# Window attention on two head pairs at once: scores of four heads in quarters of TensorE's array

## The chip, the cores and the metric

The kernel runs on one core of a Trainium2 chip. The metric is the device time of one execution in microseconds. The kernel before takes 718.71 us (median of three runs, 718.19 to 719.21). PE is the matmul engine (TensorE), DVE the vector engine, ACT the scalar engine, POOL the general engine (GpSimd); SP issues most of the DMAs.

## The reference

Three layers in a row: causal attention with a window of 64 positions (4 sequences of 576 positions, 8 heads of 64), a feed-forward layer of 512 to 2048 to 512 for all 2304 tokens, and a second one of 512 to 1024 to 512 with a softmax-weighted activation and a layer norm. All in float32.

```python
scores = q @ k^T / 8                               # per sequence and head, 576 x 576
scores = where(0 <= row - col < 64, scores, -1e9)  # a query sees itself and 63 keys before it
attn = softmax(scores)
x = attn @ v                                       # heads side by side: 2304 x 512
h = x @ w_in                                       # 2304 x 2048
g = where(h >= 1, h, where(h <= -1, 0, (h + 1)**2 / 4))
x = g @ w_out                                      # 2304 x 512
h = x @ w_in2; s = h * softmax(h)
out = layer_norm(s) * g_ln @ w_out2
```

## The kernel before, in words

The attention is worked off in *groups*. A group is a tile of 192 positions (12 tiles, `TT`) and a pair of heads (4 pairs, `NP`), so there are 48 groups, counted by `g`; a group's queries stand in three blocks of 64, and each block sees 128 keys (its own 64 and the 64 before). The first block of a sequence sees 64 keys only (`first`). The stages of a group:

- `st_qkt` brings queries and keys into transposed form, head dimension on the partitions, two heads on 128 partitions. The first three tiles do it with TensorE (L324) and copies out of PSUM (L327 to L329), the others with DVE's transposes from a special DMA layout (L314, L316). The queries are written into `q_diag`, a block-diagonal tile that is zeroed once: 64 columns of the first head filled on the upper 64 partitions, 64 columns of the second on the lower.
- `st_s` multiplies (L342): one product of 128 rows contracted, 128 stationary columns (2 heads x 64 queries) and 128 moving columns (keys) per block. The zeros of `q_diag` keep the heads apart. DVE adds the mask and takes the row's extreme (L350), ACT takes the exponential and its sum (L356).
- `st_norm` divides by the sum (L366 to L375), `st_t` transposes the weights with TensorE (L388, L390) and copies them (L393, L395), `st_v` multiplies with the values (L409): two products of 64 stationary columns per block, one per head, which write the upper and the lower 64 partitions of the output. ACT and DVE split the result into two parts `xh` and `xl` (L416, L417).

A product of float32 operands stands in the trace as two weight loads and two matmuls, here called passes: 144 score products give 288 rows of L342.

The MoE layer goes over blocks of 384 tokens (`j`, 6 blocks) and chunks of 128 hidden units (`f`, 16 chunks): 12 matmuls for a chunk (L429, three products of split operands for four parts of the contraction), the activation (ACT L438, L439, DVE L444, ACT L445, DVE L449), and 12 matmuls for the output two chunks later (L460). The first chunks are done in two halves of 192 tokens so that they can start before the second tile's attention is ready. In the first block the weights are also converted: ACT L130, DVE L134 and L135, ACT L143, POOL L144.

The order of the work: a prologue runs the first groups (`G0` = 6) stage by stage; from then on a generator, `slots`, gives out the attention in quarter steps, two of them per MoE chunk (`slot`). A scheduler then orders each engine's instructions, so that the order on an engine is near to, but not the same as, the order in the code. PSUM has eight banks: four hold the MoE output, and from the second block on the other four are a ring (`at_bank`, `h_bank`) that scores, values, transposes and MoE chunks take in turn.

Of the kernel before, what the change touches and what calls it, by code (L numbers as in the profile page):

```python
# [20 lines left out]
def kernel(  # L21
# [12 lines left out]
    nc = tc.nc  # L34
# [17 lines left out]
    G0, F0, NC, NQ, NV = 6, 2, 4, 6, 7  # L52
# [198 lines left out]
    qn, kn, qk, vw, qT, kT, xh, xl = {}, {}, {}, {}, {}, {}, {}, {}  # L251
    sc, pr, sums, pT = {}, {}, {}, {}

    def load_qk(g):
# [3 lines left out]
        if g < NPE:  # L261
# [10 lines left out]
            for h0, h1 in ((0, 2), (2, H)) if t == 0 else ((0, H),):  # L272
# [8 lines left out]
        for src, r0, m0 in ((q, tl * TT, 0), (k, tl * TT - back, 6)):  # L281
# [19 lines left out]

    q_diag = [at_p.tile([128, QB, 2, 64], F32, bufs=1, name=f"q_diag{z}") for z in range(2)]
    for z in q_diag:
        nc.vector.memset(z, 0.0)

    def st_qkt(g):
        t, hp = divmod(g, NP)
        qt = qT[g] = q_diag[g % 2]
        kt = kT[g] = at_p.tile([128, TT + 64], F32, tag="kT", name="kT")
        if g >= NPE:  # L310
            a = qk.pop(g)
            for x in range(2):
                s_ = slice(64 * x, 64 * x + 64)
                nc.vector.transpose(qt[s_, :, x, :], a[s_, 0:6, :].rearrange("p m c -> p (m c)"))  # L314
            c0 = 0 if t % TPB else 64
            nc.vector.transpose(kt[:, c0:], a[:, 6:14 - c0 // 32, :].rearrange("p m c -> p (m c)"))  # L316
            return
        ps = at_bank("ps_t")
        c = 0
        for src in (qn, kn):  # L320
# [5 lines left out]
        psq = ps[:, 0:TT].rearrange("c (i q) -> c i q", i=QB)  # L326
# [7 lines left out]
    def st_s(g):  # L334
        t, hp = divmod(g, NP)
        ps = at_bank("ps_s")
        tmp = p = at_p.tile([128, QB, 128], F32, tag="p", bufs=3, name="p")
        mx = at_p.tile([128, QB], F32, tag="mx", name="mx")
        sm = at_p.tile([128, QB], F32, tag="sm", name="sm")
# [8 lines left out]
        for i in range(QB):  # L348
            c0 = 64 if first(t, i) else 0
            nc.vector.tensor_tensor_reduce(  # L350
                out=tmp[:, i, c0:], in0=ps[:, i * 128 + c0:i * 128 + 128], in1=mask[:, c0:],
                scale=-0.125, scalar=3.0e38, op0=ALU.add, op1=ALU.min, accum_out=mx[:, i:i + 1],
            )
        for i in range(QB):
            c0 = 64 if first(t, i) else 0
            nc.scalar.activation(  # L356
                p[:, i, c0:], tmp[:, i, c0:], ACTF.Exp, bias=mx[:, i:i + 1], scale=-1.0,
                accum_out=sm[:, i:i + 1],
            )
        pr[g], sums[g] = p, sm  # L360

    def st_norm(g):
        t, hp = divmod(g, NP)
        p, sm = pr[g], sums.pop(g)
# [3 lines left out]
        eng = nc.gpsimd if g < NPE else nc.vector  # L368
# [12 lines left out]
    def st_t(g):  # L381
        t, hp = divmod(g, NP)
        p = pr.pop(g)
# [12 lines left out]
        pT[g] = o  # L396

    def st_v(g):
# [506 lines left out]
```

## Time and profile before

| | |
|---|---|
| time, median of 3 runs | 718.71 us |
| profiled execution, first to last instruction | 717.6 us |
| PE busy | 697.3 us (97%), 4259 matmuls |
| DVE busy | 455.7 us (64%) |
| ACT busy | 417.2 us (58%) |
| POOL busy | 194.3 us (27%) |

The profiled execution's own time is its span of 717.6 us; the median of the runs is 1.1 us longer. A PE that is busy 97% of the time is not at its peak, since a matmul's record runs from its start to the end of its last column while the next one has already begun; the distance between starts is what a matmul costs in a row of its like. The busy shares are means over stages with different limits, so the stages are read apart below.

### The profile page before, as it was taken

The numbers are of one execution on the slowest core, as the hardware profiler recorded it, in microseconds if no ns is written. First come the engines' busy times: TensorE is split into PE (matmuls) and PEld (weight loads), VectorE is DVE, ScalarE is ACT, GpSimd is POOL, SyncE is SP. The second block draws the span as 40 slices with busy tenths as digits, with TensorE's granted clock in tenths as the row PEclk, the third lists the DMA queues.
The fourth block names the chain that finished last, engine by engine and source line by source line (L and its number), as shares of the span: only waits on it lengthen the run. The fifth ranks groups of instructions, "written<-read, shape, count | busy, mean of one in ns | idle before, by whom it ended". The sixth has DMA issues, their size and how long they took to land.

```text
span 717.6 us, 12382 instructions
## 1 busy us (share of the span) xinstructions
PE 697.3 (97%) x4259; PEld 640.5 (89%) x4259; DVE 455.7 (64%) x1222; ACT 417.2 (58%) x1021; POOL 194.3 (27%) x217
## 2 busy tenths in 40 slices
PE   7899889999999999999999999999999999999998
PEld 5689878999999999999999999989998888888887
DVE  4549998564556556655566543463368889988850
ACT  5778877555556555666665655454454645545541
POOL 2458877200002000012002101662274132310000
PEclk9989999999999999999999999999999999999999
DMA  9985897624234252336342200644005445553421
GB/s 197 212 241 174 221 244 178 123 63 106 70 78 138 51 127 56 84 96 152 62 117 92 71 30 31 228 140 147 0 19 186 163 162 176 180 171 109 143 74 44
DMA packets 155542, 88.91 MB, mean 124 GB/s; under 512 B 118616, under 2 KB 141400, under 8 KB 155480
## 3 DMA queue, kind: packets, MB, share of 16 engines
q1 hardware_dynamic: 144040, 64.00, 35.3%
q0 software_dynamic: 8704, 19.41, 8.2%
q10 hardware_dynamic: 2736, 4.72, 1.8%
q8 instruction: 33, 0.54, 0.3%
q14 instruction: 29, 0.24, 0.1%
HBM read 63.97 MB, written 24.12 MB: 123 GB/s over the span
## 4 chain that ended last, share of the span: by engine, by line
PE 80%; issue 7%; DVE 6%; POOL 3%; ACT 2%; DMA 1%; SPq 0%; DVEq 0%; POOLq 0%; ACTq 0%
PE ps_h L429 22%; PE acc L460 22%; PE ps_o L746 14%; PE P L631 10%; PE ps_s L342 5%; PE ps_x L409 4%; PE ps_p L390 2%; POOL wil L247 2%; DVE wst L135 1%; DVE wst L134 1%; DVE gl L449 1%; ACT p L356 1%; PE ps_t L324 1%; DMA qk<-in_q_dram 1%; DVE u L444 0%
## 5 line engine op out<-in xcount | busy, mean ns | idle before, releaser
L429 PE MATMUL ps_h<-xh,wih 128*128 128x384 f32 (+1 forms) x392 | 133.3, 340 | 4.0 <-DVE u L444 4.0
L429 PE MATMUL ps_h<-xl,wih 128*128 128x384 f32 (+1 forms) x392 | 132.1, 337 | 1.4 <-DVE xl L417 1.4
L460 PE MATMUL acc<-gl,woh 128*128 128x384 f32 (+1 forms) x392 | 131.2, 336 | 2.0 <-DVE gl L449 1.6
L429 PE MATMUL ps_h<-xh,wil 128*128 128x384 f32 (+1 forms) x392 | 131.7, 336 | 0.0
L460 PE MATMUL acc<-gh,wol 128*128 128x384 f32 (+1 forms) x392 | 129.8, 333 | 0.0
L444 DVE SCALAR_TENSOR_TENSOR u<-u,ps_h 128x384 f32<-128x384 f32 (+1 forms) x98 | 53.3, 544 | 117.1 <-ACT u L439 116.9
L460 PE MATMUL acc<-gh,woh 128*128 128x384 f32 (+1 forms) x392 | 126.7, 342 | 0.0
L438 ACT ACTIVATE u<-ps_h,half 128x384 f32<-128x384 f32 (+1 forms) x98 | 56.1, 574 | 90.7 <-PE ps_h L429 86.9
L429 PEld LDWEIGHTS ps_h<-xh,wih 128*128 128x128 f32 x392 | 75.1, 192 | 5.6 <-DVE u L444 5.0
L445 ACT CAST gh<-u 128x384 fp32r<-128x384 f32 (+1 forms) x98 | 49.7, 507 | 49.3 <-DVE u L444 40.9
L429 PEld LDWEIGHTS ps_h<-xl,wih 128*128 128x128 f32 x392 | 75.2, 192 | 2.2 <-DVE xl L417 2.0
L460 PEld LDWEIGHTS acc<-gl,woh 128*128 128x128 f32 x392 | 73.8, 188 | 3.7 <-DVE gl L449 2.2
L449 DVE TENSOR_TENSOR gl<-u,gh 128x384 fp32r<-128x384 f32 x80 | 54.4, 680 | 35.1 <-ACT gh L445 34.6
L429 PEld LDWEIGHTS ps_h<-xh,wil 128*128 128x128 f32 x392 | 75.1, 191 | 0.0
L460 PEld LDWEIGHTS acc<-gh,wol 128*128 128x128 f32 x392 | 73.7, 188 | 0.1
L460 PEld LDWEIGHTS acc<-gh,woh 128*128 128x128 f32 x392 | 72.4, 188 | 0.5
L631 PE MATMUL P<-wih,x2p 128*128 128x512 f32 x216 | 70.5, 390 | 0.5 <-DVE xo L472 0.5
L356 ACT ACTIVATE p<-p,mx 128x128 f32<-128x128 f32 (+1 forms) x144 | 55.7, 389 | 17.4 <-DVE mx L350 17.4
L746 PE MATMUL ps_o<-woh,wol 128*128 128x512 f32 (+1 forms) x152 | 57.8, 380 | 0.0
L746 PE MATMUL ps_o<-woh,woh 128*128 128x512 f32 (+1 forms) x152 | 57.7, 379 | 0.0
L746 PE MATMUL ps_o<-wol,woh 128*128 128x512 f32 (+1 forms) x152 | 57.5, 378 | 0.0
L439 ACT ACTIVATE u<-u 128x384 f32<-128x384 f32 (+1 forms) x98 | 51.0, 520 | 2.3
(114 smaller groups left out, 1291.2 us busy)
## 6 DMA issues: line engine op xcount, KB each, us to landing
vw<-in_v_dram SPq DMA_DIRECT2D x32, 256.0 KB, 5.0
wst<-in_moe_w_in_dram SPq DMA_DIRECT2D x16, 512.0 KB, 5.0
wst<-in_moe_w_out_dram SPq DMA_DIRECT2D x16, 512.0 KB, 5.0
lnd<-e SPq DMA_DIRECT2D x16, 512.0 KB, 2.7
lT<-lnd SPq DMA_DIRECT2D x64, 128.0 KB, 2.9
x2d<-xo POOLq DMA_DIRECT2D x24, 192.0 KB, 2.3
out_dram<-o ACTq DMA_DIRECT2D x17, 256.0 KB, 2.8
wst<-in_moe_w_in_dram POOLq DMA_DIRECT2D x8, 512.0 KB, 5.5
```

Of the source, the lines that this page charges most:

```text
L342: nc.tensor.matmul(ps[:, i * 128 + c0:i * 128 + 128], qT[g][:, i, :, :].rearrange("p x q -> p (x q)"), kT[g][:, i * 64 + c0:i * 64 + 128], ...
L356: nc.scalar.activation(p[:, i, c0:], tmp[:, i, c0:], ACTF.Exp, bias=mx[:, i:i + 1], scale=-1.0, accum_out=sm[:, i:i + 1],)
L409: nc.tensor.matmul(ps[64 * x:64 * x + 64, i * 64:i * 64 + 64], vw[t, i][0:n, 2 * hp + x, :], o[0:n, i, 64 * x:64 * x + 64], start=True, st ...
L429: nc.tensor.matmul(ps, a, bb[:, kc, c], start=(n == 0), stop=(n == 3 * KC - 1))
L438: nc.scalar.activation(u, ps, ACTF.Relu, bias=half, scale=0.5)
L439: nc.scalar.activation(u, u, ACTF.Square)
L444: g = nc.vector.scalar_tensor_tensor(u, u, 1.0, ps, op0=ALU.min, op1=ALU.max)
L445: return nc.scalar.copy(hi, u).ins, g.ins
L449: eng.tensor_tensor(lo, u, as_f32(hi), op=ALU.subtract)
L460: nc.tensor.matmul(acc[j, e][:, c], a, bb, start=(f == 0 and n == 0 and c.start == 0), stop=(f == NF - 1 and n == 2),)
L631: nc.tensor.matmul(ps, l, r, start=(n == 0), stop=(n == 5))
L746: nc.tensor.matmul(ps, a[kk // 4][:, kk % 4, :], b[kk][:, c:c + w], start=(n == 0), stop=(n == 3 * NK2 - 1),)
```

## The change

The attention goes over *pairs* of groups: `P` counts 24 of them, each a tile of 192 positions and four heads (two head pairs `c`, two heads `x` in each). `q_diag` is gone. Keys and queries of a group now stand in one tile `kqT` (256 and 192 columns, two heads on 128 partitions), so that DVE transposes them in one instruction. For each block of 64 queries `st_s` issues four products that contract over 64 rows: head `x` has its rows on partitions 64x to 64x + 63, head pair `c` writes PSUM partitions 64c to 64c + 63, and the two `x` write two different PSUM banks. The weights `p` are then kept per `x`, with the two head pairs on the upper and the lower partitions. The values' products of two groups write one bank, and `xh` and `xl` are made for both in one instruction each.

```diff
-    G0, F0, NC, NQ, NV = 6, 2, 4, 6, 7
+    PR0, F0 = 3, 2
...
-            for h0, h1 in ((0, 2), (2, H)) if t == 0 else ((0, H),):
+            for h0, h1 in ((0, 4), (4, H)) if t == 0 else ((0, H),):
...
     def st_qkt(g):
         t, hp = divmod(g, NP)
-        qt = qT[g] = q_diag[g % 2]
-        kt = kT[g] = at_p.tile([128, TT + 64], F32, tag="kT", name="kT")
+        z = kqT[g] = at_p.tile([128, KQ + TT], F32, tag="kqT", name="kqT")
+        c0 = 0 if t % TPB else 64
         if g >= NPE:
             a = qk.pop(g)
-            for x in range(2):
-                s_ = slice(64 * x, 64 * x + 64)
-                nc.vector.transpose(qt[s_, :, x, :], a[s_, 0:6, :].rearrange("p m c -> p (m c)"))
-            c0 = 0 if t % TPB else 64
-            nc.vector.transpose(kt[:, c0:], a[:, 6:14 - c0 // 32, :].rearrange("p m c -> p (m c)"))
+            nc.vector.transpose(z[:, c0:], a[:, c0 // 32:, :].rearrange("p m c -> p (m c)"))
             return
...
-        nc.vector.tensor_copy(qt[0:64, :, 0, :], psq[0:64])
-        nc.scalar.copy(qt[64:128, :, 1, :], psq[64:128])
-        nc.scalar.copy(kt[:, TT + 64 - (c - TT):], ps[:, TT:c])
+        nc.scalar.copy(z[:, c0:KQ], ps[:, c0:KQ])
+        nc.vector.tensor_copy(z[:, KQ:], ps[:, KQ:KQ + TT])
...
+    def st_s(P):
+        t, h2 = divmod(P, NPR)
+        ps = [at_bank("ps_s") for _ in range(2)]
...
         for i in range(QB):
             c0 = 64 if first(t, i) else 0
-            nc.tensor.matmul(
-                ps[:, i * 128 + c0:i * 128 + 128],
-                qT[g][:, i, :, :].rearrange("p x q -> p (x q)"),
-                kT[g][:, i * 64 + c0:i * 64 + 128],
-                start=True, stop=True,
-            )
+            for c in range(2):
+                z = kqT[2 * P + c]
+                for x in range(2):
+                    r = slice(64 * x, 64 * x + 64)
+                    nc.tensor.matmul(
+                        ps[x][64 * c:64 * c + 64, i * 128 + c0:i * 128 + 128],
+                        z[r, KQ + i * 64:KQ + i * 64 + 64],
+                        z[r, i * 64 + c0:i * 64 + 128],
+                        start=True, stop=True,
+                    )
...
+        ps = at_bank("ps_x")[:, 0:2 * TT].rearrange("p (c n) -> p c n", c=2)
+        o = [pT.pop((P, x)) for x in range(2)]
+        for c in range(2):
+            for i in range(QB):
+                n = 64 if first(t, i) else 128
+                for x in range(2):
+                    nc.tensor.matmul(
+                        ps[64 * x:64 * x + 64, c, i * 64:i * 64 + 64],
+                        vw[t, i][0:n, 4 * h2 + 2 * c + x, :],
+                        o[x][0:n, i, 64 * c:64 * c + 64],
+                        start=True, stop=True,
+                    )
+        k2, c = slice(2 * h2, 2 * h2 + 2), slice(tj * TT, tj * TT + TT)
+        nc.scalar.copy(xh[j][:, k2, c], ps)
+        nc.vector.tensor_tensor(xl[j][:, k2, c], ps, as_f32(xh[j][:, k2, c]), op=ALU.subtract)
...
     def slots():
-        for g in range(G0 + 1, GB + 1):
-            st_s(g)
-            yield
...
+        for P in range(PB + 1, NPP + 1):
...
+            st_v(P - 1)
+            v_ahead(P)
+            if P < NPP:
+                st_t(P, 0)
+            yield
+            qkt_and_loads(2 * P + 3)
+            yield
+            yield
+            yield
+            if P < NPP:
+                st_t(P, 1)
+            if P + 1 < NPP:
+                st_s(P + 1)
+            yield
+            if P + 1 < NPP:
+                st_norm(P + 1, 0)
+                st_norm(P + 1, 1)
+            yield
+            qkt_and_loads(2 * P + 4)
             yield
```

The prologue now runs four pairs instead of seven groups before the MoE layer's slots begin, and a pair takes eight slots where a group took four.

On PE in the steady part, in the second half of the attention, the order before is this for two groups (`ps_x` are the values' products, `ps_p` the transposes of the weights, `ps_s` the scores, `acc` and `ps_h` the MoE layer):

```order
L460 MATMUL acc_2994<-gh,wol_715 128x384
L409 MATMUL ps_x<-pT,vw 64x64 x6
L390 MATMUL ps_p<-ident,p 128x128 x3
L342 MATMUL ps_s<-kT,q_diag_124 128x128 x3
L460 MATMUL acc_2991<-gh,woh_797 128x384
...
L460 MATMUL acc_2994<-gh,wol_864 128x384
L409 MATMUL ps_x<-pT,vw 64x64 x6
L390 MATMUL ps_p<-ident,p 128x128 x3
L342 MATMUL ps_s<-kT,q_diag_125 128x128 x3
L460 MATMUL acc_2991<-gh,woh_940 128x384
```

And this is the same place after the change, for one pair:

```order
L456 MATMUL acc_3019<-gh,wol_397 128x384
L405 MATMUL ps_x<-pT,vw 64x64 x12
L385 MATMUL ps_p<-ident,p 128x128 x3
L425 MATMUL ps_h<-xh,wih_553 128x384
...
L456 MATMUL acc_3019<-gh,wol_545 128x384
L385 MATMUL ps_p<-ident,p 128x128 x3
L335 MATMUL ps_s<-kqT 64x128 x12
L425 MATMUL ps_h<-xh,wih_787 128x384
```

Every 48 MoE products there is one visit of the attention, as before; but values and scores of two groups now stand in turns, twelve values' products at one visit and twelve quarter products of the scores at the next, instead of six and three at each.

On DVE at the same place, the order before holds this for one group (`p,mx<-ps_s,mask` is the mask and extreme, `u` and `gl` belong to the MoE layer):

```order
L350 ISA p,mx<-ps_s,mask 128x128
...
L314 STREAM_TRANSPOSE q_diag_125<-qk 64x3x64 x2
L316 STREAM_TRANSPOSE kT<-qk 128x256
L366 TENSOR_SCALAR sm<-sm 128x3
L367 RECIPROCAL rs<-sm 128x3
L375 TENSOR_TENSOR p<-p,rs 128x384
L444 SCALAR_TENSOR_TENSOR u<-u,ps_h 128x384
```

After the change it holds this for one pair, behind six rows of `p,mx` in a run:

```order
L345 ISA p,mx<-ps_s,mask 128x128
L345 ISA mx 128x1
L308 STREAM_TRANSPOSE kqT<-qk 128x448
L361 TENSOR_SCALAR sm<-sm 128x3
L362 RECIPROCAL rs<-sm 128x3
L370 TENSOR_TENSOR p<-p,rs 128x384
...
L370 TENSOR_TENSOR p<-p,rs 128x384
L440 SCALAR_TENSOR_TENSOR u<-u,ps_h 128x384
```

Three transposes per group have become one, and the MoE layer's `u` stands behind six maxima and two scalings instead of three and one.

## Rows read from the trace of the kernel before

**Rows 1.** Page, part 4: chain that ended last, shares of the span.

```profile
PE 80%; issue 7%; DVE 6%; POOL 3%; ACT 2%; DMA 1%; SPq 0%; DVEq 0%; POOLq 0%; ACTq 0%
PE ps_h L429 22%; PE acc L460 22%; PE ps_o L746 14%; PE P L631 10%; PE ps_s L342 5%; PE ps_x L409 4%; PE ps_p L390 2%; POOL wil L247 2%; DVE wst L135 1%; DVE wst L134 1%; DVE gl L449 1%; ACT p L356 1%; PE ps_t L324 1%; DMA qk<-in_q_dram 1%; DVE u L444 0%
```

**Rows 2.** By stretch: us; busy (count) of PE, PEld, DVE, ACT, POOL; clock; DMA.

```profile
0.00:38.00 38.00, 29.71 (x186) 24.65 (x187) 17.28 (x84) 25.53 (x89) 14.17 (x27) 0.95 0.99 210
...
60.00:112.00 52.00, 46.20 (x295) 42.24 (x294) 49.86 (x99) 40.70 (x99) 40.74 (x30) 0.97 0.88 233
...
130.00:450.00 320.00, 320.00 (x2202) 307.49 (x2201) 178.50 (x579) 189.34 (x503) 36.23 (x53) 1.00 0.35 86
450.00:717.60 267.60, 262.25 (x1282) 229.22 (x1280) 181.21 (x370) 130.46 (x244) 78.62 (x86) 1.00 0.39 130
```

**Rows 3.** Chain of waits, 298 to 301 us: start, us, what.

```profile
298.00 0.87 PE acc L460 x5
298.87 0.50 PE ps_x L409 x12
299.37 0.48 PE ps_p L390 x3
299.84 0.67 PE ps_s L342 x6
```

**Rows 4.** PE timeline, 298.4 to 300.8 us: start, us, instructions merged.

```profile
298.80 0.57 PE L409 MATMUL ps_x<-pT,vw 128*64 128x64 f32 x12
...
299.68 0.83 PE L342 MATMUL ps_s<-kT,q_diag 128*128 128x128 f32 x6
```

**Rows 5.** PE timeline at 146.6 us, one values product alone.

```profile
146.63 0.33 PE L409 MATMUL ps_x<-pT,vw 128*64 128x64 f32 x2
146.89 0.44 PE L460 MATMUL acc<-gl,woh 128*128 128x384 f32 x1
147.17 0.34 PE L460 MATMUL acc<-gh,wol 128*128 128x384 f32 x1
```

**Rows 6.** PE timeline at 306.7 us, two values products.

```profile
306.69 0.34 PE L409 MATMUL ps_x<-pT,vw 128*64 128x64 f32 x4
```

**Rows 7.** PE groups by shape, 130 to 450 us: count, busy, mean ns.

```profile
L342 PE MATMUL ps_s<-kT,q_diag 128*128 128x128 f32 x170 | 24.7, 277 | 0.0
...
L342 PE MATMUL ps_s<-kT,q_diag 128*128 128x64 f32 x16 | 2.7, 248 | 0.0
```

**Rows 8.** DVE groups by shape, whole span.

```profile
L350 DVE CUSTOM_DVE_ANT_0 p<-ps_s,mask 128x128 f32<-128x128 f32 x128 | 30.8, 287 | 18.7 <-PE ps_s L342 18.6
...
L314 DVE STREAM_TRANSPOSE q_diag<-qk 64x192 f32<-64x192 f32 x72 | 26.7, 370 | 1.1
...
L657 DVE TENSOR_TENSOR u<-P,u 128x512 f32<-128x512 f32 x27 | 18.4, 682 | 0.9 <-PE P L631 0.6
L417 DVE TENSOR_TENSOR xl<-ps_x,xh 128x192 fp32r<-128x192 f32 x48 | 16.9, 353 | 11.3 <-ACT xh L416 11.2
...
L316 DVE STREAM_TRANSPOSE kT<-qk 128x256 f32<-128x256 f32 x24 | 10.7, 446 | 0.7
```

**Rows 9.** ACT groups by shape, whole span.

```profile
L328 ACT COPY q_diag<-ps_t 64x192 f32<-64x192 f32 x12 | 3.8, 315 | 6.7 <-DVE q_diag L327 6.5
```

**Rows 10.** DVE groups, 60 to 112 us.

```profile
L314 DVE STREAM_TRANSPOSE q_diag<-qk 64x192 f32<-64x192 f32 x8 | 3.0, 370 | 0.1
...
L316 DVE STREAM_TRANSPOSE kT<-qk 128x192 f32<-128x192 f32 x4 | 1.5, 376 | 0.1
```

**Rows 11.** PE timeline at 13.8 us, early scores.

```profile
13.79 1.65 PE L342 MATMUL ps_s<-kT,q_diag 128*128 128x64 f32 x6 [0.33 <-ACT kT L329]
```

**Rows 12.** Page, part 5: the MoE chunk's three steps.

```profile
L444 DVE SCALAR_TENSOR_TENSOR u<-u,ps_h 128x384 f32<-128x384 f32 (+1 forms) x98 | 53.3, 544 | 117.1 <-ACT u L439 116.9
...
L438 ACT ACTIVATE u<-ps_h,half 128x384 f32<-128x384 f32 (+1 forms) x98 | 56.1, 574 | 90.7 <-PE ps_h L429 86.9
...
L439 ACT ACTIVATE u<-u 128x384 f32<-128x384 f32 (+1 forms) x98 | 51.0, 520 | 2.3
```

More of the change, by code (lines that the diff above doesn't have):

```diff
@@ L354, in st_s @@
[L354 to L364, printed above, removed]
+            for c in range(2):
[8 more added lines that the diff above has]
+                    )
@@ new lines, in st_s @@
+        for x in range(2):
+            p = at_p.tile([128, QB, 128], F32, tag="p", bufs=4, name="p")
+            for i in range(QB):
+                c0 = 64 if first(t, i) else 0
+                nc.vector.tensor_tensor_reduce(
+                    out=p[:, i, c0:], in0=ps[x][:, i * 128 + c0:i * 128 + 128], in1=mask[:, c0:],
+                    scale=-0.125, scalar=3.0e38, op0=ALU.add, op1=ALU.min, accum_out=mx[:, x, i:i + 1],
+                )
+            for i in range(QB):
+                c0 = 64 if first(t, i) else 0
+                nc.scalar.activation(
+                    p[:, i, c0:], p[:, i, c0:], ACTF.Exp, bias=mx[:, x, i:i + 1], scale=-1.0,
+                    accum_out=sm[:, x, i:i + 1],
+                )
+            pr[P, x], sums[P, x] = p, sm[:, x, :]
@@ L395, in st_t, with st_v @@
         nc.scalar.copy(o[:, i0:, :], ps[:, i0 * 128:QB * 128].rearrange("p (i c) -> p i c", c=128))
-        pT[g] = o
-    def st_v(g):
-        t, hp = divmod(g, NP)
+        pT[P, x] = o
+    def st_v(P):
+        t, h2 = divmod(P, NPR)
         j, tj = divmod(t, TPJ)
-        if hp == 0 and tj == 0:
+        if h2 == 0 and tj == 0:
             xh[j] = wk_p.tile([128, KC, NB], F32R, tag="xh", name="xh")
             xl[j] = wk_p.tile([128, KC, NB], F32R, tag="xl", name="xl")
-        ps = at_bank("ps_x")
-        o = pT.pop(g)
-        for i in range(QB):
-            n = 64 if first(t, i) else 128
-            for x in range(2):
-                nc.tensor.matmul(
-                    ps[64 * x:64 * x + 64, i * 64:i * 64 + 64],
-                    vw[t, i][0:n, 2 * hp + x, :],
-                    o[0:n, i, 64 * x:64 * x + 64],
-                    start=True, stop=True,
-                )
-        c = slice(tj * TT, tj * TT + TT)
-        nc.scalar.copy(xh[j][:, hp, c], ps[:, 0:TT])
-        nc.vector.tensor_tensor(xl[j][:, hp, c], ps[:, 0:TT], as_f32(xh[j][:, hp, c]), op=ALU.subtract)
+        ps = at_bank("ps_x")[:, 0:2 * TT].rearrange("p (c n) -> p c n", c=2)
+        o = [pT.pop((P, x)) for x in range(2)]
+        for c in range(2):
+            for i in range(QB):
+                n = 64 if first(t, i) else 128
+                for x in range(2):
+                    nc.tensor.matmul(
[3 more added lines that the diff above has]
+                        start=True, stop=True,
+                    )
+        k2, c = slice(2 * h2, 2 * h2 + 2), slice(tj * TT, tj * TT + TT)
+        nc.scalar.copy(xh[j][:, k2, c], ps)
+        nc.vector.tensor_tensor(xl[j][:, k2, c], ps, as_f32(xh[j][:, k2, c]), op=ALU.subtract)
     hps, gh, gl, acc = {}, {}, {}, {}
@@ L496 @@
     st_qkt(1)
-    for n in range(G0 + 4):
-        if n <= G0:
+    for n in range(PR0 + 2):
+        if n <= PR0:
             st_s(n)
-        if 1 <= n <= G0 + 1:
-            st_norm(n - 1)
-        if 0 <= n - 2 <= G0:
-            st_t(n - 2)
-        if n == NQ:
+        if n < PR0:
+            st_qkt(2 * n + 2)
+            st_qkt(2 * n + 3)
+        if n >= 1:
+            for x in range(2):
+                st_norm(n - 1, x)
+            for x in range(2):
+                st_t(n - 1, x)
+        if n == 3:
             after(load_qk, 2 * NP)
-        if n == NV:
             after(load_v, 2)
-        if n + 2 <= G0 + 1:
-            st_qkt(n + 2)
-        if 0 <= n - 3 < G0:
-            st_v(n - 3)
-        if n >= NC:
+        if n >= 2:
+            st_v(n - 2)
+            w_conv()
+            w_load(1)
             w_conv()
@@ L515 @@
     del spare[:]
-    GB = TPJ * NP * 2
+    PB = TPJ * NPR * 2
     def qkt_and_loads(m):
```

90 lines of the change are left out of this document (41 added, 49 removed).

## The prediction

> **What bounds the kernel now.** I read the chain of waits first, then busy time by stretch, then TensorE's timeline at a few places, and last the groups by shape. On the chain PE holds 80% of the span, and the attention's part of it is small: scores (L342) 5%, values (L409) 4%, transposes of the weights (L390) 2% [rows 1]. The stretches tell three regimes apart [rows 2]. From 130 to 450 us PE is busy for 320.00 of 320.00 us while DVE works 178.5 and ACT 189.3: every nanosecond taken from PE there is taken from the time. From 60 to 112 us DVE is the bound (49.9 of 52.0) and PE has 5.8 us of slack. Before 38 us nothing is full (29.7, 17.3 and 25.5 of 38 us): PE, DVE and ACT wait for one another. After 450 us there is no attention, so I give that stretch no change.
>
> **What a group of two heads costs PE today.** In the steady part the chain spends 0.50 us on the values' products, 0.48 on the transposes and 0.67 on the scores of each group, and nothing between [rows 3]. The scores are six passes (three products, two passes each) of 0.112 us: 0.67/6. The values' twelve passes start within 0.57 - 0.22 = 0.35 us (the 0.22 is a pass from start to end), 29 ns per pass, though a pass of the 128-column scores takes 112 [rows 4, 7]. Half of 112 is 56, for 64 columns; so two passes are under way at once. The cleanest sight of it: a values product that stood alone (two passes) lasted 0.33 us [rows 5], and two products side by side (four passes) 0.34 us [rows 6]. The second product goes to other columns of the array, and it costs almost nothing beside the first.
>
> Entering and leaving such a divided array is not free. 0.35 us of spacing stand against 0.50 on the chain: 0.15 us to enter. The three transposes behind take 0.48 where three passes of 0.112 would take 0.34: about 0.15 us to leave. Into a product of the MoE layer leaving is dearer: 0.26 us to its start and 0.28 to the next [rows 5], 0.54 where 0.117 + 0.174 would do (0.174 is 0.87/5 of rows 3), so 0.20 to 0.25; I take 0.20.
>
> **The change on PE, from 130 us on.** Rows 7 hold 170 + 16 = 186 score passes here. At 0.112 and half of it that is 19.0 + 0.9 = 19.9 us.
> - After: a set is one block of 64 queries of four heads: four quarter products with two passes of 128 columns each. If the four quarters run side by side as two halves do today, a set is 2 x 0.112 + three starts 7 ns apart = 0.24 us, against 0.45 for the two full products that it replaces. The new order has 180 quarters left past the same point of the MoE work: 41 sets of full width and 4 of half: 41 x 0.24 + 4 x 0.13 = 10.4. In three pairs the twelve quarters are cut as 7, 3 and 2, which begins one set more each: + 0.7. So 11.1, and -8.8 us.
> - Entering and leaving: 37 divided stretches before (30 leave to transposes, 7 to the MoE): 37 x 0.15 + 30 x 0.15 + 7 x 0.20 = 11.5. After, by the order, 16 for values (twice as long) and 22 for scores, 15 leaving to transposes and 23 to the MoE: 38 x 0.15 + 15 x 0.15 + 23 x 0.20 = 12.6. So +1.1. The first block of a sequence contracts over 64 rows and changes the division inside the values' stretch; that happens 12 times instead of 8, and I price it like an entry: +0.6.
> - One group more lies ahead of this point than before, so six transposes (6 x 0.112) and six values products (6 x 0.058) move out: -1.0, to be paid earlier.
> Sum of the stretch: -8.8 + 1.1 + 0.6 - 1.0 = -8.1 us.
>
> **The change elsewhere.** DVE loses two transposes of 0.370 and one of 0.446 per group and gains one of 448 columns [rows 8]. By the slope between 192 and 256 columns (68 ns per 64) that is about 0.65, so -0.54 us per group. The two xl subtractions of 0.353 become one of 384 columns; between 0.353 at 192 and 0.682 at 512 [rows 8] it is 0.55, -0.16 per pair. ACT loses the second copy of the queries (12 x 0.315) [rows 9]. From 130 us on neither is full, so this is worth nothing; the cover is PE's 320 of 320 us, and the six maxima, six exponentials and two scalings of a pair, now in one run, have the 24 MoE products (4.2 us) twice before they are needed.
>
> Up to 112 us DVE's relief counts. Eight transposes of 0.370 and four of 0.376 stand in the bound stretch [rows 10], 4.5 us; four of 384 columns at 0.58 take 2.3. Against it one more group is worked off before 130 us: three maxima of 0.287 with their read-outs, its scaling and its transposes, which I put at 2 us of DVE and as much of ACT. Counted over the new order to the 18th MoE chunk, DVE has 3 us less, ACT 0.4 less, PE 1 us more (17 score stretches, six of them against a values stretch, many cut 6 and 6). At the start the first load brings four heads in place of two, 4 x 98 KB before the first transpose; the pair then waits for both. On the other hand early score passes are slow: six within 1.65 us, 0.21 us a pass [rows 11], and halving these is on the chain. I take -1.5 us for all up to 130 us, bounds -5 (DVE's relief and the early scores in full) and +5 (the chain lengthens by one load, one group and the extra entries).
>
> **Sum.** 717.6 - 8.1 - 1.5 = 708.0 for the profiled execution's span. The runs' median, 718.7, stands 1.1 above that span, so 709.1; I forecast 709.
>
> **A rule against the change.** Rows 5 and 6 show two column halves at once; no row shows row halves or four quarters. The Trainium skill ("TensorE: Matmul & The Clock Gate", section "Part 3: Packing small matmuls — row/col tiling") says that matmuls start and end strictly in program order, and that a pack of tiles spans one matmul's duration plus about 4 ns per further tile. Its first half is at odds with rows 5 and 6 as I read them, its second half fits them. What strict order would do is the first rival below.
>
> **Rivals.**
> 1. *Only one neighbour overlaps.* Two passes of one quarter must follow each other on the same quarter. If passes start only in program order, the second pass of each quarter holds up the rest, and a set is 4 x (0.112 + 0.007) = 0.48 us. The stretch from 130 us would then cost 41 x 0.48 + 4 x 0.26 + 0.7 = 21.4 against 19.9: +1.5 + 1.1 + 0.6 - 1.0 = +2.2; before 130 us PE gains some 5 us of work, 1 to 2 of which show after DVE's relief. 718.7 + 2.2 + 1.3 = 722. For it: nothing shows that a third and fourth product may pass two waiting ones. Against it: under it four values passes (rows 6) would need 0.11 + 0.06 us more than the two of rows 5, and they needed 0.01. It decides once a set takes over 0.24 + 9.6/45 = 0.45 us: there the gain is gone. This is the case on the other side.
> 2. *Quarters that exclude each other* (one at a time): a set takes 0.90, 45 sets add 27 us to the forecast's stretch, less what DVE covers early: about 740.
> 3. *The start eats part of it*: the quarters work, but the first 130 us go to the bad bound: 709 + 6.5 = 715.5.
> 4. *Banks.* From the second MoE block on scores, transposes, values and MoE chunks share four PSUM banks in turn, and a pair's scores now take two at once. The next chunk then needs the bank of a chunk whose three steps (0.574, 0.520, 0.544 [rows 12]) and 24 products lie in between: 2.1 + 0.5 + 0.7 us of PE work against 1.6. That fits; if six maxima of 0.29 got in front of the last step it would be 0.5 us late in each of some 15 pairs: 716.5.
>
> **Chances.** Forecast 0.63; rival 1 0.14; rival 2 0.05; rival 3 0.09; rival 4 0.07; the remaining 0.02 for the pieces not working as described (no change). The forecast's own range is 704 to 714; rivals 3 and 4 lie inside 717 and rival 1 at 718 to 724. A range of 703 to 721 leaves out rival 2, half of rival 1 and the far side of the early bound. Within 0.2% (1.4 us, what a measurement can tell from none) counts as the same. Faster 0.77 (forecast and most of 3 and 4), same 0.05, slower 0.18 (1 and 2).
>
> **What would show it.** A score stretch of twelve quarters whose 24 passes start within about 0.7 us (rival 1: 1.4; rival 2: 2.7), in groups of four some 7 ns apart. 0.15 us at its entry and 0.2 behind it. PE without idle time from 130 to 440 us, the attention gone some 8 us earlier, and the stretch after it as long as before. In the bound stretch from 60 us DVE still full but ending earlier. Wrong would be: PE waiting for DVE's u behind a pair's maxima, or the first dense MoE products later than today's 38 us by more than 3 us.

## The result, and the profile after

The changed kernel takes 727.5 us (median of 4 runs, 727.07 to 727.98); the kernel before, on the same chip, 718.96. The ratio is 1.0119, 95% interval 1.0104 to 1.0133: slower by 8.5 us, where 709 was forecast. The profiled span went from 717.6 to 726.1 us.

First the chain of waits, as in [rows 1]: PE falls from 80% to 76% of it, DVE rises from 6 to 9% and DMA from 1 to 5%. Waits have come in that were not there before.

```profile
PE 76%; DVE 9%; DMA 5%; ACT 4%; issue 3%; POOL 2%; SPq 1%; DVEq 0%; POOLq 0%; ACTq 0%
```

Then the stretches of [rows 2], with the same columns:

```profile
0.00:38.00 38.00, 26.16 (x224) 18.95 (x225) 18.97 (x87) 22.63 (x80) 15.94 (x28) 0.97 1.03 221
60.00:112.00 52.00, 44.53 (x329) 40.04 (x324) 41.07 (x81) 37.21 (x87) 33.53 (x27) 0.97 0.81 214
130.00:450.00 320.00, 318.56 (x2427) 302.42 (x2426) 161.56 (x507) 188.74 (x489) 39.16 (x56) 1.00 0.36 86
```

From 60 to 112 us DVE works 41.07 us instead of 49.86: the engine that was the bound now stands idle for 11 us, and PE works 1.7 us less as well. No engine is full there any more. What fell on DVE are mainly the weight conversions, here one of their two lines before and after (last before the bar the count; then us in total, mean ns):

```profile
L135 DVE SCALAR_TENSOR_TENSOR wst<-wst 128x512 uint32<-128x512 uint32 x18 | 24.3, 1355 | 0.2
L135 DVE SCALAR_TENSOR_TENSOR wst<-wst 128x512 uint32<-128x512 uint32 x16 | 16.9, 1062 | 1.2 <-ACT wst L130 0.5
```

With L134 it is 38.6 us before and 29.7 after. The transposes that the change was to save there fell as forecast, from 4.5 to 2.3 us.

Fixed times cut through different work in the two kernels, so the next table goes by the work itself: when the matmul with that number of the first MoE layer (L425 and L456 after, L429 and L460 before, 2352 in all) starts, and how long PE has been idle by then, both counted in the traces.

| MoE matmul | before, us | after, us | difference | PE idle before | after |
|---|---|---|---|---|---|
| 20th | 39.4 | 37.5 | -1.9 | 8.3 | 11.8 |
| 50th | 44.7 | 46.8 | +2.1 | 8.3 | 13.0 |
| 100th | 56.6 | 63.1 | +6.5 | 9.1 | 16.1 |
| 200th | 81.4 | 86.9 | +5.5 | 11.6 | 18.4 |
| 250th | 92.3 | 104.6 | +12.3 | 11.6 | 23.5 |
| 500th | 152.7 | 167.4 | +14.7 | 14.9 | 27.6 |
| 2000th | 463.4 | 469.8 | +6.4 | 14.9 | 27.6 |
| 2350th | 535.5 | 541.5 | +6.0 | 16.5 | 28.9 |
| end of span | 717.6 | 726.1 | +8.5 | | |

So three things happened. Up to the 500th matmul 14.7 us are lost, 12.7 of them PE standing idle. From there to the 2000th 8.3 us come back. At the end another 2.5 go. The same cut by stretch, first before, then after (columns as above; span less PE's busy time is its idle time):

```profile
0.00:152.70 152.70, 137.79 (x941) 125.17 (x942) 110.78 (x326) 110.46 (x319) 83.23 (x84) 0.97 0.80 193
152.70:463.40 310.70, 310.70 (x2117) 299.47 (x2117) 167.95 (x534) 182.30 (x471) 40.46 (x56) 1.00 0.36 90
```

```profile
0.00:167.40 167.40, 139.80 (x1087) 121.29 (x1088) 109.86 (x312) 111.03 (x312) 80.97 (x84) 0.96 0.73 178
167.40:469.80 302.40, 302.40 (x2259) 289.00 (x2258) 152.34 (x451) 177.75 (x444) 39.34 (x56) 1.00 0.37 92
```

**The quarters work.** PE's timeline at 300 us, answering to [rows 3, 4]:

```profile
300.04 0.49 PE L385 MATMUL ps_p<-ident,p 128*128 128x128 f32 x3
300.46 0.89 PE L335 MATMUL ps_s<-kqT 64*64 64x128 f32 x24
301.28 0.45 PE L425 MATMUL ps_h<-xh,wih 128*128 128x384 f32 x1
301.56 0.34 PE L425 MATMUL ps_h<-xl,wih 128*128 128x384 f32 x1
```

From the first score pass to the next product 0.82 us pass, for four heads. Before, two heads took 0.59 by the same measure, from 299.68 us [rows 4] to the next product:

```profile
300.27 0.42 PE L460 MATMUL acc<-gh,woh 128*128 128x384 f32 x1
```

Inside, the trace has the starts of four passes 6, 7 and 7 ns apart. The next four start 160 ns after the first four in the first set, and 109 ns after them in the others, so from the second set on a set of four quarters takes 0.22 us.

**Where PE waits.** The longest waits of PE between 38 and 145 us (us in total, times, longest; 14.3 us in all; before there were 6.5 in this window, 4.0 of them for the MoE step u):

```profile
PE ps_p L383 <- DVE p L366: 4.2, 3, 2.1
PE ps_s L335 <- DVE mx L345: 2.8, 1, 2.8
PE ps_p L385 <- POOL p L370: 2.7, 2, 1.6
PE ps_t L316 <- DVE kqT L319: 1.1, 1, 1.1
```

All of these are waits of the attention. On the timeline, with the wait in brackets:

```profile
52.30 0.60 PE L316 MATMUL ps_t<-ident,qkn 128*128 128x128 f32 x4 [1.09 <-DVE kqT L319]
54.52 0.55 PE L385 MATMUL ps_p<-ident,p 128*128 128x128 f32 x3 [1.61 <-POOL p L370]
```

```profile
91.78 0.77 PE L335 MATMUL ps_s<-kqT 64*64 64x64 f32 x12 [2.81 <-DVE mx L345]
...
95.87 0.30 PE L383 MATMUL ps_p<-ident,p 128*64 128x128 f32 x1 [1.52 <-DVE p L366]
...
97.44 0.66 PE L385 MATMUL ps_p<-ident,p 128*128 128x128 f32 x2 [0.75 <-DVE p L370]
```

At 91.78 us the scores of a pair wait for a PSUM bank that DVE has not read out. And DVE itself, in the same window, waits for weights:

```profile
DVE wst L135 <- ACT wst L130: 5.7, 5, 3.0
DVE wst L134 <- DMA wst<-in_moe_w_out_dram: 5.5, 3, 3.7
...
DVE wst L134 <- DMA wst<-in_moe_w_in_dram: 1.9, 2, 1.1
```

Before, DVE waited for no weight load there, and 0.7 us for ACT's step on one. How such a wait and the banks come together shows at 62 us. DVE reads the first bank of a pair out from 62.80 us, and the pair's second bank only from 69.41; a conversion that waits for its load stands between them:

```profile
62.80 0.28 DVE L345 CUSTOM_DVE_ANT_0 p<-ps_s,mask 128x128 f32<-128x128 f32 x1
...
68.57 0.43 DVE L134 TENSOR_SCALAR wst<-wst 128x512 uint32<-128x512 uint32 x1 [3.73 <-DMA wst<-in_moe_w_out_dram]
...
69.41 0.25 DVE L345 CUSTOM_DVE_ANT_0 p<-ps_s,mask 128x128 f32<-128x128 f32 x1
```

The next two pairs have 7.3 us each between their two banks (90.99 to 98.32 and 113.04 to 120.33 us). SP's queue shows what stands in front of the weight loads (start, us, what; here the queue after):

```profile
51.12 0.37 SPq L122 DMA_DIRECT2D wst<-in_moe_w_in_dram  x1
52.66 1.78 SPq L286 DMA_DIRECT2D qk<-in_q_dram  x4
54.48 1.89 SPq L286 DMA_DIRECT2D qk<-in_k_dram  x4
56.50 1.81 SPq L286 DMA_DIRECT2D qk<-in_q_dram  x4
58.75 1.79 SPq L286 DMA_DIRECT2D qk<-in_k_dram  x4
60.64 1.84 SPq L286 DMA_DIRECT2D qk<-in_q_dram  x4
62.52 1.89 SPq L286 DMA_DIRECT2D qk<-in_k_dram  x4
64.51 0.39 SPq L124 DMA_DIRECT2D wst<-in_moe_w_out_dram  x1
```

Twenty-four loads of queries and keys stand in a row; for 13.4 us no weight load starts. Before, the same loads began at 64.69 us with a weight load between every two to eight of them.

**The end.** Behind the MoE layer there is one wait that the profile before doesn't have, behind a DRAM read of x2 that landed 6.43 us after its issue:

```profile
574.94 6.43 DMA x2r<-x2d
...
586.07 4.15 PE ps_o L762 x17
```

PE stood 2.16 us before that row.

### The profile page after: what moved, and what is told of

Read it like the earlier page. It is cut to its first block, busy times and chain, and to the rows that moved or that the text cites. A ratio compares the mean times of both kernels' runs of the same rounds, so it can differ in the third digit from the quotient of the medians.

```text
span 726.1 us, 12842 instructions
## 1 busy us (share of the span) xinstructions
PE 690.8 (95%) x4547; PEld 626.1 (86%) x4547; DVE 435.6 (60%) x1124; ACT 413.2 (57%) x985; POOL 192.3 (26%) x217
## 4 chain that ended last, share of the span: by engine, by line
PE 76%; DVE 9%; DMA 5%; ACT 4%; issue 3%; POOL 2%; SPq 1%; DVEq 0%; POOLq 0%; ACTq 0%
PE acc L456 24%; PE ps_h L425 24%; PE ps_o L762 12%; PE P L647 7%; PE ps_s L335 3%; PE ps_x L405 3%; PE ps_p L385 2%; DMA wst<-in_moe_w_out_dram 2%; DVE wst L135 2%; DVE wst L134 1%; DMA qk<-in_k_dram 1%; DVE gl L445 1%; DMA x2r<-x2d 1%; DMA wst<-in_moe_w_in_dram 1%; ACT p L351 1%
## 5 line engine op out<-in xcount | busy, mean ns | idle before, releaser
L425 PE MATMUL ps_h<-xh,wih 128*128 128x384 f32 (+1 forms) x392 | 135.5, 347 | 2.2 <-DVE mx L345 1.4
L425 PE MATMUL ps_h<-xh,wil 128*128 128x384 f32 (+1 forms) x392 | 132.9, 339 | 0.6 <-POOL wil L144 0.6
L425 PE MATMUL ps_h<-xl,wih 128*128 128x384 f32 (+1 forms) x392 | 132.9, 339 | 0.2 <-DVE xl L413 0.2
L456 PE MATMUL acc<-gl,woh 128*128 128x384 f32 (+1 forms) x392 | 130.9, 334 | 1.9 <-DVE gl L445 1.3
L456 PE MATMUL acc<-gh,wol 128*128 128x384 f32 (+1 forms) x392 | 130.3, 333 | 0.0
L456 PE MATMUL acc<-gh,woh 128*128 128x384 f32 (+1 forms) x392 | 127.4, 338 | 0.0
L425 PEld LDWEIGHTS ps_h<-xh,wih 128*128 128x128 f32 x392 | 74.7, 191 | 5.6 <-issue 2.9
L456 PEld LDWEIGHTS acc<-gl,woh 128*128 128x128 f32 x392 | 73.8, 188 | 3.1 <-DVE gl L445 1.7
L425 PEld LDWEIGHTS ps_h<-xl,wih 128*128 128x128 f32 x392 | 75.3, 192 | 1.1 <-DVE xl L413 0.6
L425 PEld LDWEIGHTS ps_h<-xh,wil 128*128 128x128 f32 x392 | 75.4, 192 | 1.0 <-POOL wil L144 0.8
L456 PEld LDWEIGHTS acc<-gh,woh 128*128 128x128 f32 x392 | 73.7, 190 | 2.2 <-issue 1.4
L456 PEld LDWEIGHTS acc<-gh,wol 128*128 128x128 f32 x392 | 73.8, 188 | 0.2 <-issue 0.2
```

Of the source, the lines that this page charges most:

```text
L425: nc.tensor.matmul(ps, a, bb[:, kc, c], start=(n == 0), stop=(n == 3 * KC - 1))
L456: nc.tensor.matmul(acc[j, e][:, c], a, bb, start=(f == 0 and n == 0 and c.start == 0), stop=(f == NF - 1 and n == 2),)
```

## Two suspects and the first four runs

Theory Q: the row of loads on SP's queue holds the weights back, VectorE waits for them in order, and the attention's maxima behind it are late. Theory B: in the first MoE block attention has two PSUM banks; a pair's scores take both, and nothing else of the attention can start on PE until VectorE has read six maxima. Each is taken out of the changed kernel alone, and then both.

**Loads two groups ahead.**

```diff
-        if m >= NPE and m + 4 < NG:
-            load_qk(m + 4)
+        if m >= NPE and m + 2 < NG:
+            load_qk(m + 2)
         if m == NPE - 1:
-            for z in range(1, 5):
+            for z in range(1, 3):
```

> The changed kernel, with the query and key loads of a group issued two groups ahead of its transpose instead of four (two sets at group 11 instead of four). Theory Q (loads in front of weights on SP's queue): in the changed kernel 24 loads of groups 12 to 14 stand in one row from 52.66 to 64.46 us with no weight load between; VectorE, in order, then waits 7.4 us for weights between 38 and 145 us and holds the masked maxima behind it. Spread out, that wait goes below 2 us, TensorE's idle time up to 170 us falls from 26.8 to about 20 us, and the time from 727.5 to 719-722. Theory B (a pair's scores hold both attention banks of PSUM until VectorE has read them): the loads are beside the point, 726-729.

Measured: 726.9 us (723.13 to 729.27), ratio to before 1.0107 (1.0063 to 1.015). The edit did most of what it should: the row on SP's queue is broken up, the last weight is converted at 118.6 us instead of 126.2 (before: 123.5), and DVE's wait for weight loads falls from 7.4 to 3.5 us (expected: below 2). PE is idle for 28.5 us up to the 500th matmul all the same (27.6 in the changed kernel). Halving the wait for weights gave PE nothing back. Q alone falls.

**Value loads later.** `v_ahead(P)` moved from behind `st_v(P - 1)` to behind `st_t(P, 1)`.

> The changed kernel, with the value loads of the next tile issued at the end of a pair's round instead of right behind the V products that free their buffers. Theory Q: SP stands 5.6 us at the value load of 86.33 us with weight loads behind it; moved, this wait shrinks, -1 to -3 us (724.5-726.5), the burst of query and key loads stays. Theory B: no change, 726.5-728.5.

Measured: 726.76 us, 1.0102 (1.0082 to 1.0121), with 27.7 us of idle time by the 500th matmul. That is 0.7 us under the changed kernel, no more than the runs of one kernel differ.

**One bank at a time.**

```diff
-        ps = [at_bank("ps_s") for _ in range(2)]
+        one = P <= 8
...
         for x in range(2):
+            if one:
+                scores((x,))
```

> The changed kernel, where the first nine pairs take one PSUM bank at a time: the quarters of the upper heads of both groups (two side by side), their masked maxima, then the same for the lower heads; from the tenth pair on all four quarters as before. The nine pairs pay 12 more starts of some 0.1 us each on TensorE, at most 9 x 0.7 = 6 us if TensorE bounds there. Theory B: the waits of TensorE for banks (ps_s 2.8, ps_p 7.6, ps_t 1.6, ps_x 0.8 us between 38 and 145 us) shrink by half and more, 720-724. Theory Q: the waits for weights stay, 727-733.

Measured: 722.3 us (720.3 to 725.92), 1.0046 (1.0023 to 1.0069), 5.2 us less than the changed kernel. B is a cause, and the place fits: at the 250th matmul, where the changed kernel is 12.3 us late, this one is 2.7 late, and at the 350th it is at 117.2 us, level with the kernel before (117.8). By the 500th it is 9.4 us late again, 5.82 of them in a single wait. Its chain (start, us, what) shows what is late there:

```profile
107.61 5.90 DMA wst<-in_moe_w_out_dram
...
114.99 1.26 DVE wst L134
...
119.29 1.44 DVE wst L134
...
120.84 1.59 DVE wst L135
122.43 2.63 DVE p L376
...
125.20 0.40 PE ps_p L393
```

A weight load lands at 113.5 us, VectorE then converts weights nearly without a break up to 122.4 us, and the scaling L376 for which PE waits stands behind them in its order. With the banks out of the way the late weights seem to matter; but 2.63 us of the chain are L376 itself, which takes 0.23 us as a rule (last section).

**All three.**

> The three edits together. Theory Q alone: as loads two groups ahead with later value loads, 717-721. Theory B alone: 720-724. Both: 711-717, which would beat the kernel before (718.7).

Measured: 719.78 us (717.35 to 726.19), 1.0013 (0.999 to 1.0037): 7.7 us less than the changed kernel, level with the kernel before. PE is idle 20.9 us up to the 500th matmul, which starts at 158.1 us. That is above the 711 to 717 expected if each cause paid in full. Against one bank at a time alone it is 2.5 us less, but the two intervals (1.0023 to 1.0069 and 0.999 to 1.0037) overlap, so what the loads add is not shown.

## The same two put into the kernel before

If these are the causes, they must cost the kernel before as much. `m == NPE - 3` with `range(3, 7)` in place of `m == NPE - 1` with `range(1, 5)` puts the same 24 loads in a row on its queue. And its scores go to two banks:

```diff
-        ps = at_bank("ps_s")
+        pa = at_bank("ps_s")
+        pb_ = at_bank("ps_s") if g <= 16 else pa
...
         for i in range(QB):
+            ps = pb_ if i else pa
...
```

> The kernel before, with the four sets of query and key loads of groups 12 to 15 issued two groups earlier, so that 24 loads stand in one row on SP's queue with no weight load between, as in the changed kernel. Nothing else is changed. Theory Q or A (the row of loads holds the weights): 721-725. Theory B (banks only): 718-719.5.

> The kernel before, where the scores of one group of the first 17 lie in two PSUM banks (first block of queries in one, the other two in the other) instead of one, so that they hold both attention banks until the maxima are read, as a pair's do in the changed kernel; TensorE's work is the same. Theory B or A: 721-726. Theory Q (loads only): 718-720.

> The kernel before with both: the row of 24 loads and scores in two banks. Theory A: at least the larger of the two alone, 723-730, which would be the whole early loss of the changed kernel put into the kernel before. If the two have nothing to do with it: 718-720.

| kernel before with | us | ratio (interval) | 500th MoE matmul, us | PE idle by then |
|---|---|---|---|---|
| nothing changed | 718.8 | | 152.7 | 14.9 |
| the row of loads | 723.32 | 1.0065 (1.0044 to 1.0086) | 153.1 | 16.0 |
| scores in two banks | 728.99 | 1.0138 (1.0103 to 1.0172) | 161.5 | 21.1 |
| both | 727.40 | 1.0127 (1.0098 to 1.0156) | 160.2 | 19.8 |

The two banks cost 10.2 us, with not one instruction more on PE. The stretch up to the 500th matmul has 8.8 of them:

```profile
0.00:161.50 161.50, 140.41 (x940) 126.40 (x941) 111.62 (x326) 112.87 (x319) 82.21 (x84) 0.93 0.77 182
```

6.2 us of the 8.8 us lost are idle time. The other 2.6 are busy time, with the same instructions: the granted clock of this stretch (third number from the end) is 0.93 where it was 0.97. Its longest waits are for the attention again:

```profile
134.99 0.30 PE L391 MATMUL ps_p<-ident,p 128*64 128x128 f32 x1 [1.91 <-DVE p L374]
...
139.97 0.87 PE L393 MATMUL ps_p<-ident,p 128*128 128x128 f32 x3 [1.79 <-DVE p L378]
...
142.93 0.69 PE L432 MATMUL ps_h<-xh,wih 128*128 128x384 f32 x1 [0.81 <-DVE mx L353]
```

and behind them the granted clock falls to a mean of 0.55 over ten microseconds, most of them at 1.2 GHz instead of 2.4:

```profile
130.00:140.00 10.00, 6.16 (x48) 5.03 (x49) 6.78 (x30) 4.80 (x20) 2.74 (x5) 0.77 0.56 136
140.00:150.00 10.00, 9.19 (x45) 8.34 (x46) 3.84 (x17) 4.05 (x12) 0.00 (x0) 0.55 0.66 138
```

This is not the loss of the changed kernel at the same place. At the 350th matmul the kernel with two banks is at 112.2 us, 5.6 ahead of the kernel before, with less of the attention done; then it falls back. The scheduler had also made another order of the same instructions: from 131.83 to 142.93 us no MoE product stands on PE, but 46 passes of the attention in a row, where the kernel before has at most 21 between the 50th and the 500th matmul. So the run shows what two banks cost together with the order that came with them. Two banks in the old order were not run.

The row of loads costs the time expected, 4.5 us, but its profile doesn't show it where it was expected: only 0.4 us is lost by the 500th matmul, and 2.5 us at a wait at 540 us that grew from 0.49 to 2.96. There too PE's order differs: behind the last MoE product two products L631 stand ahead of the wait, and eight in the kernel before. The two edits don't add up either. So B is shown from both sides, in different places of the early stretch; Q is at most an accomplice, and no run shows it clear of noise in the changed kernel.

## A finer step, which did not help

A third idea: the pair is too coarse a step for engines that take their instructions in a fixed order. Scores, maxima, norm and transposes were taken apart into upper and lower heads, each in a slot of its own, in the prologue too, as the kernel before does with groups.

> The changed kernel, where the prologue and the first MoE block's rounds go by half pairs, as the kernel before goes by groups: scores of the upper heads into one bank, their maxima, norm and transposes a step apart from those of the lower heads; loads as in the changed kernel. Theory G (a pair at a time is too coarse for two banks and in-order engines): TensorE's idle time up to the 500th matmul of the MoE layer, 27.6 us in the changed kernel, 25.0 us with one bank at a time and 14.9 us before, falls to 17-20 us, and the time to 715-719. Theory B (only the banks were at fault, and the previous run has already taken that out): as that run, 721-723. Theory Q (the loads): the same 721-723.

> The same kernel again for one more profile of its own: if the early idle time is set by the order of the instructions, its 38 to 145 us look the same; if it is set by when transfers land, TensorE's idle time up to the 500th matmul differs by over 2 us.

> Half pairs, query and key loads two groups ahead, and the first tile's loads in three pieces (two, two and four heads) so that the first transposes can start on two heads. Theory G: as half pairs alone, -1 to -2 us for the start (first transpose at 2.75 us, not 4.60) and -1 to -3 us for the spread loads: 711-716. Theory Q: the loads were the cause, -5 us and more against half pairs alone. If neither the start nor the loads matter: as half pairs alone within 1 us.

> Half pairs (one bank at a time, as in the run by half pairs) and query and key loads two groups ahead, the first tile's loads as in the changed kernel. The run by half pairs alone still had the 24 loads in a row in front of the weights (no weight load from 55.9 to 71.5 us) and lost 16.2 us from the 50th to the 75th matmul of the MoE layer, where the kernel before takes 7.8. Theory A (either of two causes, banks or late weights, is enough to stop the in-order engines, so both must go): 716-720. Rival S (in-order bunching that neither edit touches): 722-725, as half pairs alone.

Measured: 724.25 (1.0068, 1.0047 to 1.009) for half pairs, 723.71 for one more run and profile of them, 726.33 (1.0101) with spread loads and a start in three pieces, 725.96 (1.009, 1.0064 to 1.0117) with spread loads alone. All times missed. PE's idle time up to the 500th matmul did fall, to 21.4, 21.7, 23.8 and 23.4 us, but its busy time rose to some 143 us (137.1 with one bank at a time). Behind waits the clock fell; two rows of the half pairs, at 0.66:

```profile
40.00:50.00 10.00, 8.43 (x45) 8.03 (x45) 5.06 (x10) 5.56 (x14) 5.71 (x5) 0.66 0.80 262
...
60.00:70.00 10.00, 7.71 (x57) 6.61 (x57) 5.97 (x13) 5.96 (x18) 8.28 (x7) 0.66 0.31 50
```

The second profile has the same idle time within 0.3 us at the 500th matmul, which speaks for the order as the reason and against the landing of transfers. With the first tile in three pieces the 20th MoE matmul starts at 42.3 us instead of 37.8; four more loads stand ahead of the first weights, which I take to be the reason. What holds the half pairs between the 50th and 75th matmul (16.2 us, before 7.8) was not settled; PE waits there for POOL's scaling and for maxima by turns.

## Two quarters instead of four

> One bank at a time (two quarters side by side, not four) for all 24 pairs and not for the first nine only. It measures the term of the steady stretch: if four quarters side by side are worth what the forecast put (8.8 us over the stretch of 15 pairs, some 0.6 us a pair), the time is 722.3 + 8 to 9 = 730-732, and the gain of TensorE from the 500th to the 2000th matmul goes from -8 us to about 0. If the steady gain came from elsewhere (fewer reductions and copies on VectorE), it stays 721-724.

Measured: 726.77 us (722.93 to 728.34), 1.0112 (1.0095 to 1.0129), between the two expectations. From the 500th to the 2000th matmul PE takes 306.0 us, against 302.4 with four quarters and 310.7 before:

```profile
159.30:465.30 306.00, 306.00 (x2259) 292.62 (x2259) 148.96 (x448) 177.96 (x442) 39.34 (x56) 1.00 0.37 91
```

So four quarters side by side instead of two are worth 3.6 us of the steady gain of 8.3. The forecast's -8.8 for the passes rested on the same difference (a set in 0.24 instead of 0.45 us). More than half of the gain comes from elsewhere; some 1.6 us of it are work done before the 500th matmul (see below).

## The early stretch as before, pairs afterwards

If the whole loss lies in the first block, a kernel that keeps the groups there and goes over to pairs afterwards must gain. It is the kernel before, with block-diagonal queries, up to group 17; from group 18 (`GL`) on `st_s2` and `st_v2` are the changed kernel's `st_s` and `st_v`:

```diff
+            if g >= GL:
+                qt = qT[g] = q_diag[g % 2].rearrange("p i x q -> p (i x q)")[:, 0:TT]
+                nc.vector.transpose(qt, a[:, 0:6, :].rearrange("p m c -> p (m c)"))
...
+        for P in range(GL // 2, NPP + 1):
```

> The kernel before up to its group 17, in the same order on every engine up to the start of the second MoE block (block-diagonal queries, one group at a time, one bank for its scores), and pairs in quarters from group 18 on. Theory A (the steady stretch gains what was forecast, and the whole loss lies in the first 170 us, from what the pair does to banks, queue and order): the early stretch as before (500th matmul of the MoE layer at 152.7 +- 1 us), the gain of the steady stretch kept (-6 to -8 us), 710-713. Rival T (the loss comes with the pairs wherever they are, or the end loses it again): 717-722.

Measured: 712.94 us (710.75 to 713.33), ratio 0.9900 (0.9884 to 0.9915). It beats both kernels: 6.5 us under the kernel before, 15.4 under the changed one on the same chip. Its 500th matmul starts at 150.1 us, 2.6 earlier than in the kernel before and outside the +-1 us expected, though the code is the same up to the second MoE block; the profile is of its fastest run, 2.2 us under the median. The steady stretch keeps the gain, 8.7 us up to the 2000th matmul:

```profile
0.00:150.10 150.10, 131.88 (x952) 119.54 (x953) 109.78 (x322) 110.11 (x319) 83.02 (x84) 0.97 0.83 197
150.10:452.10 302.00, 302.00 (x2286) 289.90 (x2285) 151.68 (x493) 179.94 (x456) 40.34 (x56) 1.00 0.37 93
```

Theory A holds: the pair pays where PE is the bound, and costs where the engines wait for one another.

Two more runs were made beside it. The changed kernel again:

> The changed kernel again, for a second profile: the single wait of 2.2 us at 586 us, for a DRAM read that landed in 6.4 us instead of 3.7 to 4.5, is tied to the change if it stands in this profile too, and chance if it doesn't. The time itself 726-728.5. If the early loss is set by the order, TensorE is idle 26-28.5 us up to the 500th matmul again.

728.33 us (1.0115, 1.0097 to 1.0132); 27.9 us of idle time by the 500th matmul; and the wait at the end stands there again, 2.16 us at 587.44. It isn't chance. The hybrid has 1.82 us at the same place, the scores in two banks of the kernel before 1.16: it doesn't go with the pairs alone, and what sets it stays open.

The tenth pair's scores a slot earlier, ahead of the ninth pair's second transposes, on top of the three edits:

> The three edits together (one bank at a time in the first nine pairs, loads two groups ahead, value loads later), and the scores of the tenth pair issued one slot earlier, ahead of the transposes of the ninth, so that their maxima are read before the second MoE block asks for banks. In the run with the three edits TensorE stood 1.44 us there and the granted clock of the next 10 us was 0.83. Theory B: -1.5 to -3 us against that run (717-718.5). If the wait only moves: 719-721.

719.72 us (1.0015, 0.9993 to 1.0038), the same as without. The wait where the second block asks for banks went from 1.44 to 0.57 us, and two others of 1.34 and 0.90 us came in at 88 and 93 us. The wait only moved.

## Why the prediction was wrong

**The steady stretch was right in its sum.** Forecast -8.1 us; measured -8.3 between the 500th and the 2000th matmul, PE without a gap in both kernels. A set of four quarters takes 0.22 us (forecast 0.24), so rivals 1 and 2 are out. The rule of the Trainium skill weighed there ("TensorE: Matmul & The Clock Gate", "Part 3: Packing small matmuls — row/col tiling", strict order of starts) did not come true as rival 1 applied it to these two-pass products: as I read the starts, the fourth quarter's first pass comes 20 ns after the first one's, ahead of the first one's second pass, 160 ns after it. The trace doesn't tell in which order the passes were issued, so the rule itself is not refuted. The rule's other half, some 4 ns for each further tile, comes near the 6 to 7 measured.

**Its terms were not.** The distances from each start to the next, added up by product from the 500th to the 2350th matmul (entries and leaving inside, idle time left out): scores 16.2 us before and 11.7 after, values 16.7 and 14.5, transposes of the weights 10.8 and 9.6, MoE products 328.1 and 327.4. Of the scores' 4.5 us, 1.2 are two groups that had been scored earlier, of the transposes' 1.2 some 0.4 are one group. So the scores gained 3.3 us, the values 2.2, the transposes 0.8 and the MoE products 0.7: 7.0 in all, where the forecast had 8.8 - 1.1 - 0.6 = 7.1. It had all of the 8.8 in the scores' passes, which gained 3.3 with their entering and leaving. The passes before were mis-sized: 0.67 us for two heads from the chain, where 0.59 pass from their first start to the next product's, some 2 us over 28 groups by estimate. The values, the transposes and the MoE products, from which it expected a small loss by entering and leaving, gained 3.7. Right by its sum, with errors that cancelled: that is luck.

**The step that failed is the early one**: "I take -1.5 us for all up to 130 us, bounds -5 and +5". It came to +14.7 by the 500th matmul. It summed up DVE's relief as work ("DVE has 3 us less") and took the bound engine to stay the bound. DVE did get less work, and from 60 to 112 us it stood idle for 11 of 52 us. The working asked how much each engine has to do; it did not ask who holds what while it waits. A pair holds two banks of two: with one bank at a time the changed kernel is level with the kernel before at the 350th matmul, where it had been 13.1 us late, and two banks put into the kernel before cost it 10.2 us, together with the order that came with them.

Nor was DVE full of its own work there. Of its 49.9 us in the kernel before 38.6 are 36 conversions; at the length that they have with POOL nearly idle (0.42 and 0.69 us, last section) they would be some 20 us, an estimate. Rival 3 named the place, but its bound of +5 was a longer chain at the start, and the start is not late: the 20th matmul is 1.9 us earlier.

**Rival 4 had the right resource in the wrong stretch.** It counted banks from the second MoE block on, where four are shared, and not in the first, where the attention has two. (From 130 us on PE waited for a bank only once, 1.44 us at the turn to the second block.) I had also read that SP's loads move, without counting what the 24 loads stand in front of; taking that out gave nothing by itself, and 2.5 us within noise once the banks were out of the way.

**After 450 us** I gave no change; 2.5 us were lost from the 2350th matmul on, 2.2 of them at one wait. The hybrid loses 2.6 from the 2000th on.

What of the 14.7 us is accounted for: one bank at a time takes out 5.2 us of the time, the two edits to the loads with it 7.7 together (5.3 and 9.3 at the 500th matmul, the second in a profile of that kernel's fastest run). Against the hybrid the kernel with the three edits is still 8.0 us late at the 500th matmul: 2.7 us of idle time, and 5.3 us of busy time, of which some 1.6 are two groups scored and one transposed ahead of time; most of the rest I take to be the scores at two quarters and PE's lower clock, without a run that separates them.

## What to carry to other kernels

Before batching two units of work into one step, count what the step holds (banks, staging buffers, places in a queue) in every stretch, against what there is in that stretch: where one engine is full, the saving counts; where engines wait for one another, the holding counts. A kernel whose stretches have different limits may want the batched form only in some of them. And a suspect is best tried both ways, taken out of the slow kernel and put into the fast one. Compare the scheduler's orders too: an edit to what is held can move them, and then the run shows both.

## What had not been expected of the hardware

The scaling L376 of 64 columns on VectorE takes 226 ns as a rule, but 2700 ns once, at 122.35 us in the run with one bank at a time (ns min/median/max):

```profile
L376 DVE TENSOR_TENSOR p<-p,rs x12: 219/226/2700, 87.8 to 339.1; 128x64 f32<-128x64 f32 x12
```

POOL ran two of its subtractions on SBUF operands in that time (122.42 to 125.0 us). The Trainium skill ("SBUF — State Buffer", "SBUF: two separate sides") says that VectorE, with two operands in SBUF, and GpSimd lock a shared pair of ports against each other for a whole instruction. The row agrees with it, though no run here took POOL's work away to prove it.

The conversions show the same throughout. In the kernel before, 29 of the 48 instructions L134 have tensor instructions of POOL beside them for less than a quarter of their time, and they take 0.41 to 0.43 us; the 19 others take 0.40 to 1.54. For L135 it is 0.65 to 0.70 us against 0.66 to 1.82. So part of what the profile calls busy may be waiting inside an instruction.
